# Attention and a gated feed-forward layer on one core: signs of the weights made on ScalarE, the clamp replaced by a check of sums, the closing checks split, and another order

## The chip, the cores and the metric

The kernel runs on one core of one Trainium2 chip. The metric is the device time of one execution in microseconds (us); the median of three runs before the change is 667.53 us (666.39 to 667.61). Work of the core is spread over TensorE (PE, matmuls), VectorE (DVE), ScalarE (ACT), GpSimd (POOL) and SyncE (SP, here only the queue that issues DMAs).

## The reference

```python
def _attn_ref(q, k, v, n_global, n_local):            # q, k, v: (4, 8, 768, 64)
    scores = scale * np.matmul(q, k.transpose(0, 1, 3, 2))
    keep = is_global | is_local                       # 8 first keys, or 0 <= row - key < 96
    dist = np.where(is_global & ~is_local, float(n_local), np.abs(rel))
    scores = np.where(keep, scores - slopes[:, None, None] * dist, -1e9)
    scores = scores - np.max(scores, axis=-1, keepdims=True)
    a = np.exp(scores)
    a = a / (np.sum(a, axis=-1, keepdims=True) + 1e-09)
    return np.matmul(a, v)

def _moe_ref(x, w_in, w_out):                         # x: (3072, 512), w_in: (512, 2048), w_out: (2048, 512)
    h = x @ w_in
    sp = np.where(h > 20.0, h, np.log1p(np.exp(np.minimum(h, 20.0))))
    g = h * np.tanh(sp)
    return g @ w_out
```

The weights arrive as 64-bit floats and are seen by the kernel as pairs of 32-bit words.

## The kernel before

The 3072 rows are cut into 12 chunks of 256 (`NC`), each with 8 score tiles per block of 128 rows, `t` = 0 to 95 in all. For a tile: matmuls of scores (`scores`, L370, two tiles at a time), the row maximum on DVE (`largest`, L384), the exponential with its row sum on ACT (`exps`, L393), a split of the result into two 16-bit halves (`high_a`, `low_a`), a transposing DMA (`turn_a`) and the matmuls with v (`weigh`, L429). Each block of rows then gets its normalisation (`rows`) and is split and transposed in turn (`high_x`, `low_x`, `turn_x`).

The feed-forward part runs in 96 steps `m`, 8 to a chunk, each of 256 rows by 256 of the 2048 inner columns. Step m is: 24 matmuls into the PSUM tile `ph` (`moe_in`, L474); on ACT e = exp(-h) (`exp_h`, L481); on DVE `half_e` (L485), which clamps e at 2^35 and adds 0.5; on ACT the square, a logarithm with a bias and an exponential (`square_e` L489, `ln_u` L493, `inverse_u` L497); on DVE a product with e + 0.5 (`times_r`, L501) and a product with h (`times_h`, L505, which also gives a maximum into `gmax`); a split into 16-bit halves `gt` (`high_g`, `low_g`); and 12 matmuls into `po` (`moe_out`, L523).

The weights come in 32 pieces of 128 x 512 (`load_w`), and each must be turned from 64-bit words into a pair of 16-bit halves before `moe_in` or `moe_out` reads it: `exponent_w` scales the upper word into the tile `wc`; `sign_w` writes the two 16-bit words of the tile `ws`, the low bits with a shift (L315) and the sign with a mask (L316), both on DVE; `join_w` merges `wc` and `ws` (L321, DVE); `high_w` and `low_w` make the halves. Raw pieces lie in the places of finished ones, so a later load also waits for earlier joins.

The order of all this is written out by hand in the string `PROGRAM`: one letter per function (the table `acts` gives it) and the number of the tile, step or piece, such as `i16` for `moe_in(16)`. Each engine's queue holds its instructions in that order, and an engine works its queue strictly from the front; DMAs are issued by SP's queue in the same order. A tick after a token (`g1'`) sends a function that can run on either of two engines to the other one: to DVE in place of ACT for the functions that go through `copy` (L151 on DVE, L153 on ACT), to DVE in place of POOL for those that go through `rest` (L157).

After the last step two ACT instructions per half move `po` out (`evacuate`, L530). Then the kernel decides whether its shortcuts were valid: it forms indicators of `osum`, `xmax`, `wmax` and `gmax` on DVE (L634 to L637), sums them over the partitions with one matmul (L639), reduces the result to one flag on DVE (L641 to L649, L79), loads the flag and, were it 0, would run a second, plain version (`dense`). With these inputs it does not run.

## Time and profile before

| | |
|---|---|
| median of three runs | 667.53 us (666.39 to 667.61) |
| the profiled execution | 665.3 us, of which the span from first to last instruction 663.5 us |
| PE busy, instructions | 599.8 us, 5042 matmuls |
| DVE busy, instructions | 511.1 us, 1300 |
| ACT busy, instructions | 459.5 us, 1030 |
| POOL busy, instructions | 165.4 us, 129 |
| mean granted clock of TensorE | 0.958 of full |

Groups of instructions are read as: line, engine, operation, tile out<-in, shape and type, count, then busy time in us, mean ns of one, and the idle time of the engine in front of them with what ended it. A stretch of the span is read as: its length, then busy us of each engine with the count of instructions, the granted clock of TensorE, and the share of the DMA engines. Start-to-start times on one engine are shorter than the durations shown, since consecutive instructions overlap by some tens of ns.

### The profile page before, as it was taken

What the parts mean: (1) busy time and instruction counts of PE and PEld (TensorE: products, weight loads), DVE (VectorE), ACT (ScalarE), POOL (GpSimd) and SP (SyncE); (2) the same over time, 40 slices, a digit from 0 to 9 for tenths busy, and PEclk for the clock granted to TensorE, in tenths of its full rate; (3) what the DMA queues carried; (4) which work ended last, traced back from release to release, by engine and by line L of the source; (5) the groups of instructions that cost most, each with busy time, mean ns of one, the idle gap of its engine ahead of it and who ended that gap; (6) DMA issues with size and microseconds to landing.
All of it is one profiled execution on the core that took longest, in us unless ns stands there. A gap on an engine that the chain in (4) does not pass through costs nothing.

```text
span 663.5 us, 13588 instructions
## 1 busy us (share of the span) xinstructions
PE 599.8 (90%) x5042; PEld 407.4 (61%) x5042; DVE 511.1 (77%) x1300; ACT 459.5 (69%) x1030; POOL 165.4 (25%) x129
## 2 busy tenths in 40 slices
PE   3456849997999999999999998999999999999995
PEld 2345537564767667676666666666676676667762
DVE  7789999999886897597489889796768468364551
ACT  3656765766895894786586896787776786565660
POOL 1424332413150401112132354321231203021000
PEclk9767878998999999999999999999999999999998
DMA  8999996834562683194144666741133025320001
GB/s 198 248 239 208 226 312 214 234 112 138 144 164 56 149 180 70 41 203 97 43 109 113 139 163 150 144 124 41 34 81 81 17 68 124 81 33 1 33 1 36
DMA packets 152681, 80.39 MB, mean 121 GB/s; under 512 B 121376, under 2 KB 141856, under 8 KB 152608
## 3 DMA queue, kind: packets, MB, share of 16 engines
q1 hardware_dynamic: 152608, 79.46, 49.8%
q8 instruction: 41, 0.67, 0.4%
q14 instruction: 32, 0.26, 0.1%
HBM read 38.54 MB, written 6.29 MB: 68 GB/s over the span
## 4 chain that ended last, share of the span: by engine, by line
PE 56%; DVE 7%; ACT 1%; issue 1%; DMA 1%; SPq 0%; DVEq 0%
PE ph L474 26%; PE po L523 25%; PE pav L429 3%; PE sc L370 2%; DVE r L501 1%; DVE gf L505 1%; DVE A L384 1%; DVE e L485 1%; DMA AT<-hl 1%; DVE wc L157 0%; DVE xhl L451 0%; DVE vo L219 0%; DVE vo L151 0%; ACT e L481 0%; ACT r L497 0%
## 5 line engine op out<-in xcount | busy, mean ns | idle before, releaser
L474 PE MATMUL ph<-xT,wts 128*128 128x256 f16 x2304 | 268.6, 275 | 14.5 <-DVE gmax L505 13.6
L474 PEld LDWEIGHTS <-wts 128*128 128x128 f16 x2304 | 225.4, 99 | 56.0 <-issue 13.7
L523 PE MATMUL po<-wts,gt 128*128 128x512 f16 x1056 | 241.7, 382 | 3.4 <-DVE gt L157 3.4
L523 PEld LDWEIGHTS <-gt 128*128 128x128 f16 x1152 | 110.6, 98 | 129.1 <-issue 5.1
L157 POOL TENSOR_TENSOR gt<-gf,gt 128x512 f16<-128x512 f32 x46 | 57.0, 1238 | 268.5 <-ACT gt L153 122.3
L501 DVE TENSOR_TENSOR r<-r,e 128x512 f32<-128x512 f32 x96 | 73.7, 768 | 46.2 <-ACT r L497 45.5
L393 ACT ACTIVATE A<-A,nm 128x256 f32<-128x256 f32 (+1 forms) x192 | 91.6, 478 | 20.5 <-DVE nm L384 20.2
L157 POOL TENSOR_TENSOR hl<-A,hl 128x512 f16<-128x512 f32 (+1 forms) x52 | 67.0, 1295 | 129.3 <-DVE hl L151 54.8
L481 ACT ACTIVATE e<-ph 128x512 f32<-128x512 f32 x96 | 56.4, 588 | 56.1 <-PE ph L474 55.7
L489 ACT ACTIVATE u<-e 128x512 f32<-128x512 f32 x96 | 60.1, 626 | 39.1 <-DVE e L485 39.0
L485 DVE TENSOR_SCALAR e<-e 128x512 f32<-128x512 f32 x96 | 48.4, 504 | 46.0 <-ACT e L481 45.7
L384 DVE CUSTOM_DVE_ANT_0 A<-sc,mb 128x256 f32<-128x256 f32 (+1 forms) x192 | 67.2, 395 | 8.6 <-PE sc L370 6.6
L493 ACT ACTIVATE r<-u,quarter 128x512 f32<-128x512 f32 x96 | 68.9, 718 | 2.1
L505 DVE CUSTOM_DVE_ANT_0 gf<-r,ph 128x512 f32<-128x512 f32 x96 | 65.5, 682 | 5.3 <-DVE r L501 1.6
L497 ACT ACTIVATE r<-r 128x512 f32<-128x512 f32 x96 | 59.9, 624 | 1.6
L153 ACT ACTIVATE gt<-gf 128x512 f16<-128x512 f32 x61 | 38.1, 624 | 26.5 <-DVE gmax L505 26.3
L429 PEld LDWEIGHTS <-AT 128*128 128x128 f16 x1056 | 39.6, 102 | 18.7 <-DMA AT<-hl 10.0
L370 PE MATMUL sc<-kr,qr 64*128 64x256 f32 (+1 forms) x96 | 24.3, 570 | 28.8 <-DVE nm L384 23.0
L157 DVE TENSOR_TENSOR gt<-gf,gt 128x512 f16<-128x512 f32 x50 | 39.2, 785 | 8.2 <-ACT gt L153 7.5
L157 POOL TENSOR_TENSOR wts<-ws,wts 128x512 f16<-128x512 f32 x16 | 26.8, 1676 | 67.7 <-ACT wts L153 62.6
L429 PE MATMUL pav<-vc,AT 128*128 128x64 f16 x480 | 34.3, 199 | 8.9 <-DMA AT<-hl 8.3
L429 PE MATMUL pav<-vo,AT 128*128 128x64 f16 x576 | 38.8, 199 | 0.0
(90 smaller groups left out, 542.0 us busy)
## 6 DMA issues: line engine op xcount, KB each, us to landing
kr<-kd SPq DMA_DIRECT2D x32, 208.0 KB, 4.4
qr<-qT SPq DMA_DIRECT2D x24, 256.0 KB, 4.1
vr<-v SPq DMA_DIRECT2D x12, 512.0 KB, 4.0
wts<-w_in SPq DMA_DIRECT2D x12, 512.0 KB, 5.3
wts<-w_out SPq DMA_DIRECT2D x12, 512.0 KB, 5.2
out<-ob SPq DMA_DIRECT2D x11, 512.0 KB, 3.1
vc<-vo SPq DMA_DIRECT2D x20, 192.0 KB, 2.8
kr<-kd SPq DMA_DIRECT2D x16, 144.0 KB, 3.7
```

What stands on the lines that cost most here:

```text
L157: (nc.vector if other else nc.gpsimd).tensor_tensor(out, in_, high, op=ALU.subtract)
L384: nc.vector.tensor_tensor_reduce(out=A[:, j, 0:w], in0=sc[j][:, 0:w], in1=m, scale=-1.0 / (UNIT if ci < CF32 else UNIT * SQ), scalar=3.0e3 ...
L393: nc.scalar.activation(A[:, j], A[:, j], AF.Exp, bias=nm[:, h:h + 1], scale=-1.0, accum_out=rs[:, h:h + 1])
L429: nc.tensor.matmul(pav[:, cols], AT[:, (x * 2 + j) * nk + kk, :], vs[kk][:, y, cols], start=(n == 0), stop=(n == last))
L474: nc.tensor.matmul(ph[:, j, :].rearrange("p (b t) -> p b t", b=2), wv4[:, 2 * fb, x, c * P:(c + 1) * P], xT[:, :, y * NCC + c, :], start=( ...
L481: nc.scalar.activation(mish[m]["e"], mish[m]["h"], AF.Exp, scale=-1.0 / (SV * SW))
L489: nc.scalar.activation(u, mish[m]["e"], AF.Square)
L493: nc.scalar.activation(mish[m]["r"], mish[m]["u"], AF.Ln, bias=quarter, scale=1.0 / RS)
L497: nc.scalar.activation(r, r, AF.Exp, scale=-1.0)
L501: nc.vector.tensor_tensor(r, r, mish[m]["e"], op=ALU.mult)
L505: nc.vector.tensor_tensor_reduce(out=gf, in0=mish[m]["r"], in1=mish[m]["h"], scale=SG / (SV * SW * RS), scalar=0.0, op0=ALU.mult, op1=ALU. ...
L523: nc.tensor.matmul(pos[ci][t], gt[:, x, j, t * P:(t + 1) * P], wv4[:, 2 * fb + 1, y, :], start=(fb == 0 and n == 0), stop=(fb == NFB - 1 a ...
```

## The change

Five things change.

1. `sign_w` keeps only the sign, and can run on ACT: a scaled copy of the upper word by 2^-111 into a 16-bit float leaves a zero with the sign. The shift for the low bits is its own function, `bits_w`, on DVE. Of the 32 signs 19 go to ACT and 13 stay on DVE.
2. `half_e` is gone. The 0.5 is added in two places: as the bias of the square on ACT, read from a tile `half`, and inside `times_r`, which becomes a scalar_tensor_tensor, (e + 0.5) * r. In place of the clamp, `exp_h` also gives out the sum over its row (`esum`), and the closing check asks that no sum reach 2^35.
3. The closing checks become `checks` 0, 1 and 2 inside the written order: 0 and 1 stand ahead of the last `moe_out`, with one matmul (L570) ahead of its 12, and 2 behind the evacuation, with one matmul of two columns and two DVE instructions.
4. `PROGRAM` is a new order throughout, and the ticks differ: over the whole program, ACT takes 6 more `exponent_w` and all 8 masks of the first kind (`mask_own`) and 4 more of the second (`mask_far`), DVE 14 more `high_g`.
5. The flag is written as an integer directly.

How the queues move is shown at three places. The first is DVE in the part where the weights are turned and the first feed-forward steps run. `ISA` is the custom instruction of L505 (L511 now), and L316 (before) and L320 (now) are the sign. Before:

```order
L315 TENSOR_SCALAR ws<-wts 128x512
L316 TENSOR_SCALAR ws<-wts 128x512
L501 TENSOR_TENSOR r<-r,e 128x512
L321 SCALAR_TENSOR_TENSOR ws<-wc,ws 128x512
L505 ISA gf,gmax<-r,ph 128x512
L505 ISA gmax 128x1
L157 TENSOR_TENSOR gt<-gf,gt 128x512
L321 SCALAR_TENSOR_TENSOR ws<-wc,ws 128x512
L315 TENSOR_SCALAR ws<-wts 128x512
L316 TENSOR_SCALAR ws<-wts 128x512
L485 TENSOR_SCALAR e<-e 128x512
```

And now:

```order
L320 TENSOR_SCALAR ws<-wts 128x512
L151 TENSOR_SCALAR wts<-ws 128x512
L326 TENSOR_SCALAR ws<-wts 128x512 x2
L330 SCALAR_TENSOR_TENSOR ws<-wc,ws 128x512 x2
L507 SCALAR_TENSOR_TENSOR r<-e,r 128x512
L326 TENSOR_SCALAR ws<-wts 128x512
L157 TENSOR_TENSOR wts<-ws,wts 128x512
L511 ISA gf,gmax<-r,ph 128x512
L511 ISA gmax 128x1
```

The shift (L315, now L326) no longer has a mask behind it each time, and L485 is gone between the products.

The second place is ACT in the same part of the program: L481 (now L491) is the first exponential of a step, L489 (L495) the square, L493 (L499) the logarithm, L497 (L503) the second exponential. Before:

```order
L481 ACTIVATE e<-ph 128x512
L153 ACTIVATE gt<-gf 128x512
L153 ACTIVATE wts<-ws 128x512
L489 ACTIVATE u<-e 128x512
L481 ACTIVATE e<-ph 128x512
L493 ACTIVATE r<-u,quarter 128x512
L497 ACTIVATE r<-r 128x512
```

And now:

```order
L153 ACTIVATE wc<-wts 128x512
L491 ACTIVATE e,esum<-ph 128x512
L495 ACTIVATE u<-e,half 128x512
L499 ACTIVATE r<-u,quarter 128x512
L322 ACTIVATE ws<-wts 128x512
L503 ACTIVATE r<-r 128x512
```

The square can follow the exponential with nothing of DVE between, it reads a bias, and signs (L322) stand between the instructions of a step.

The third place is the end of DVE's queue. Before, all that follows the sum over `osum` (L634) came behind the evacuation:

```order
L634 TENSOR_SCALAR ind<-osum 128x24
L641 TENSOR_SCALAR v_8666<-sc 1x48
L643 COPY v_8668<-sc 1x2
L644 TENSOR_REDUCE v_8668<-sc 1x12
L647 TENSOR_REDUCE v_8672<-v_8666 1x1
L645 TENSOR_SCALAR v_8668<-v_8668 1x14
L648 TENSOR_REDUCE v_8672<-v_8668 1x1
L649 SCALAR_TENSOR_TENSOR done<-v_8672,fl 1x1
L79 CAST done_i<-done 1x1
```

Now only the last two rows do; the reductions ahead of them wait for the matmul that stands in front of the last `moe_out`:

```order
L578 TENSOR_TENSOR v_114<-v_114 1x1
L579 TENSOR_SCALAR v_114<-v_114 1x1
L580 SCALAR_TENSOR_TENSOR v_114<-v_114,fl 1x1
L585 TENSOR_SCALAR last<-sc 1x2
L586 SCALAR_TENSOR_TENSOR done_i<-last,v_114 1x1
```

Nine instructions behind the evacuation have become two.

The diff, cut (the rows of the order are left out but for two of each):

```diff
-    def sign_w(i):
-        r = wraw[i]
-        s = mt.tile([P, DM], I32, name="ws", bufs=WB)
-        h16 = r.rearrange("p f w -> p (f w)").bitcast(U16).rearrange("p (f w) -> p f w", w=4)
-        s16 = s.bitcast(U16).rearrange("p (f w) -> p f w", w=2)
-        nc.vector.tensor_scalar(s16[:, :, 0], h16[:, :, 1], 13, None, op0=ALU.logical_shift_right)
-        nc.vector.tensor_scalar(s16[:, :, 1], h16[:, :, 3], 0x8000, None, op0=ALU.bitwise_and)
-        wst[i, 1] = s
+    def words(i, w):
+        if (i, 1) not in wst:
+            wst[i, 1] = mt.tile([P, DM], I32, name="ws", bufs=WB)
+        return wst[i, 1].bitcast(U16).rearrange("p (f w) -> p f w", w=2)[:, :, w]
+    def sign_w(i, other=False):
+        if other:
+            nc.vector.tensor_scalar(words(i, 1), halves(i, 3), 0x8000, None, op0=ALU.bitwise_and)
+        else:
+            nc.scalar.activation(words(i, 1).bitcast(F16), wraw[i][:, :, 1].bitcast(F32), AF.Copy, scale=EXPO)
+    def bits_w(i):
+        nc.vector.tensor_scalar(words(i, 0), halves(i, 1), 13, None, op0=ALU.logical_shift_right)
...
-        nc.scalar.activation(mish[m]["e"], mish[m]["h"], AF.Exp, scale=-1.0 / (SV * SW))
-    def half_e(m):
-        e = mish[m]["e"]
-        nc.vector.tensor_scalar(e, e, NTOP, 0.5, op0=ALU.min, op1=ALU.add)
+        nc.scalar.activation(mish[m]["e"], mish[m]["h"], AF.Exp, scale=-1.0 / (SV * SW), accum_out=esum[:, m:m + 1])
...
-        nc.scalar.activation(u, mish[m]["e"], AF.Square)
+        nc.scalar.activation(u, mish[m]["e"], AF.Square, bias=half_)
...
-        nc.vector.tensor_tensor(r, r, mish[m]["e"], op=ALU.mult)
+        nc.vector.scalar_tensor_tensor(r, mish[m]["e"], 0.5, r, op0=ALU.add, op1=ALU.mult)
...
+    def checks(i):
+        if i == 0:
+            nc.vector.tensor_scalar(ind[:, 0:2 * NC - 2], osum[:, 0:2 * NC - 2], 0.0, 0.0, op0=ALU.mult, op1=ALU.is_equal)
...
+        elif i == 1:
+            nc.vector.reduce_max(worst, esum, axis=AX.X)
...
+            nc.tensor.matmul(pi, ones, ind, start=True, stop=True)
...
+        else:
+            pe = ps.tile([1, 2], F32, name="sc")
+            nc.tensor.matmul(pe, ones, osum[:, 2 * NC - 2:], start=True, stop=True)
+            last = cp.tile([1, 2], F32, name="last")
+            nc.vector.tensor_scalar(last, pe, 0.0, 0.0, op0=ALU.mult, op1=ALU.is_equal)
+            nc.vector.scalar_tensor_tensor(L.done_i, last[:, 0:1], v3[:, 3:4], last[:, 1:2], op0=ALU.mult, op1=ALU.mult)
...
-        K0 q0 q1 L0' L6' L5' K1 L1' L4' M3 M2' L2' M0 L3' v0 M7' M1 M4' M5' M6' L7' f0 q2 s0 t0 t1 y0 s2 y1 g0' p0' q3 g1' t2 p1 t3 y2 X0 h0' s4 y3
+        K0 q0 K1 L7 v0 L3 L0 L6 L4 f0 L5 M3 M1' M4 M5 M6 q1 M2 M0 M7 L2 L1 s0 q2 t0 t1 y0 s2 y1 g0' p0' h0 g1' X0 t2 t3 y2 q3 p1' s4 y3 l0 X1 g2 t4 p2' y4 x0
...
-        i94 z93 Z93' i95 j94 m94 u94 n94 o91 r94 j95 G94 m95 H94 u95 n95 o92 z94' Z94 r95 G95 H95 o93 z95' Z95' o94 o95 Q11
+        o93 r95 G95 H95 o94 z95 Z95 k0 k1 o95 Q11 k2
...
-    nc.vector.tensor_scalar(ind[:, 0:2 * NC], osum, 0.0, 0.0, op0=ALU.mult, op1=ALU.is_equal)
-    nc.vector.tensor_scalar(ind[:, 2 * NC:4 * NC], xmax, 1.0, None, op0=ALU.is_ge)
-    nc.vector.tensor_scalar(ind[:, 4 * NC:NX], wmax, 1.0, None, op0=ALU.is_ge)
-    nc.vector.tensor_scalar(ind[:, NX:], gmax, 1.0, None, op0=ALU.is_ge)
-    pi = ps.tile([1, NX + NC * NFP], F32, name="sc")
-    nc.tensor.matmul(pi, ones, ind, start=True, stop=True)
...
```

More of the change, by code (lines that the diff above doesn't have):

```diff
@@ L72, in tile_kernel @@
     nlf = n_f[:, 1:2]
-    done = const.tile([1, 1], F32, name="done")
     done_i = const.tile([1, 1], I32, name="done_i")
@@ L78, in tile_kernel @@
         windowed(st, tc, locals())
-    nc.vector.tensor_copy(done_i, done)
     left = nc.values_load(done_i[0:1, 0:1], min_val=0, max_val=1)
@@ L144, in windowed @@
     nc.vector.memset(quarter, 0.25 / RS)
+    half_ = cp.tile([P, 1], F32, name="half")
+    nc.vector.memset(half_, 0.5)
     ones = cp.tile([P, 1], F32, name="ones")
@@ L334, in windowed @@
     gmax = cp.tile([P, NC * NFP], F32, name="gmax")
+    esum = cp.tile([P, NC * NFP], F32, name="esum")
     NT_ = NC * 2 * (H // 2)
@@ L543, in flags @@
         nc.vector.tensor_scalar(fl[:, 3:4], L.n_f[0:1, 1:2], float(NLMAX), fl[:, 2:3], op0=ALU.is_le, op1=ALU.mult)
+    NX = 4 * NC
+    NG = NC * NFP
+    ind = cp.tile([P, NX + NG + 1], F32, name="ind")
+    worst = cp.tile([P, 1], F32, name="worst")
+    v1 = cp.tile([1, NX - 2], F32, name="v1")
+    v2 = cp.tile([1, NC], F32, name="v2")
+    v3 = cp.tile([1, 4], F32, name="v3")
+    def checks(i):
+        if i == 0:
+            nc.vector.tensor_scalar(ind[:, 0:2 * NC - 2], osum[:, 0:2 * NC - 2], 0.0, 0.0, op0=ALU.mult, op1=ALU.is_equal)
+            nc.vector.tensor_scalar(ind[:, 2 * NC - 2:NX - 2], xmax, 1.0, None, op0=ALU.is_ge)
+            nc.vector.tensor_scalar(ind[:, NX - 2:NX], wmax, 1.0, None, op0=ALU.is_ge)
+        elif i == 1:
+            nc.vector.reduce_max(worst, esum, axis=AX.X)
+            nc.vector.tensor_scalar(ind[:, NX + NG:], worst, NTOP, None, op0=ALU.is_lt)
+            nc.vector.tensor_scalar(ind[:, NX:NX + NG], gmax, 1.0, None, op0=ALU.is_ge)
+            pi = ps.tile([1, NX + NG + 1], F32, name="sc")
+            nc.tensor.matmul(pi, ones, ind, start=True, stop=True)
+            nc.vector.tensor_scalar(v1, pi[:, 0:NX - 2], P - 0.5, None, op0=ALU.is_ge)
+            nc.vector.tensor_reduce(v3[:, 0:1], v1, axis=AX.X, op=ALU.min)
+            nc.vector.tensor_scalar(v3[:, 2:3], pi[:, NX + NG:], P - 0.5, None, op0=ALU.is_ge)
+            nc.vector.tensor_tensor(v3[:, 0:1], v3[:, 0:1], v3[:, 2:3], op=ALU.mult)
+            nc.vector.reduce_max(v2, pi[:, NX:NX + NG].rearrange("p (c f) -> p c f", f=NFP), axis=AX.X)
+            nc.vector.tensor_reduce(v3[:, 1:2], v2, axis=AX.X, op=ALU.min)
+            nc.vector.tensor_reduce(v3[:, 2:3], pi[:, NX - 2:NX], axis=AX.X, op=ALU.min)
+            nc.vector.tensor_tensor(v3[:, 1:2], v3[:, 1:2], v3[:, 2:3], op=ALU.min)
+            nc.vector.tensor_scalar(v3[:, 1:2], v3[:, 1:2], 0.5, None, op0=ALU.is_ge)
+            nc.vector.scalar_tensor_tensor(v3[:, 3:4], v3[:, 0:1], fl[:, 3:4], v3[:, 1:2], op0=ALU.mult, op1=ALU.mult)
+        else:
[4 more added lines that the diff above has]
+            nc.vector.scalar_tensor_tensor(L.done_i, last[:, 0:1], v3[:, 3:4], last[:, 1:2], op0=ALU.mult, op1=ALU.mult)
@@ L556, in windowed @@
         "R": rows, "T": high_x, "U": low_x, "V": turn_x,
-        "A": exponent_w, "B": sign_w, "C": join_w, "D": high_w, "E": low_w,
-        "i": moe_in, "j": exp_h, "m": half_e, "u": square_e, "n": ln_u, "r": inverse_u, "G": times_r, "H": times_h,
-        "z": high_g, "Z": low_g, "o": moe_out, "Q": evacuate, "Y": store, "f": lambda i: flags(),
+        "A": exponent_w, "S": sign_w, "B": bits_w, "C": join_w, "D": high_w, "E": low_w,
+        "i": moe_in, "j": exp_h, "u": square_e, "n": ln_u, "r": inverse_u, "G": times_r, "H": times_h,
@@ L560, in windowed @@
+        "z": high_g, "Z": low_g, "o": moe_out, "Q": evacuate, "Y": store, "f": lambda i: flags(), "k": checks,
     }
     PROGRAM = """
[L562 to L564 removed]
```

127 lines of the change are left out of this document (56 added, 71 removed).

## The prediction

> **What bounds the kernel now.** I read the page's busy shares and slices first, then the busy time by stretches, then PE's waits, then the groups of DVE and ACT up to 165 us. The page's parts 1 and 2 (each digit is tenths of a fortieth of the span):
>
> ```profile
> PE 599.8 (90%) x5042; PEld 407.4 (61%) x5042; DVE 511.1 (77%) x1300; ACT 459.5 (69%) x1030; POOL 165.4 (25%) x129
> PE   3456849997999999999999998999999999999995
> DVE  7789999999886897597489889796768468364551
> ```
>
> PE is the engine of the whole, but not at the front: in the first six slices (16.6 us each) DVE is fuller. The stretches, cut at points that mean something below (start:end, then us and counts of PE, PEld, DVE, ACT, POOL):
>
> ```profile
> 0.00:77.57 77.57, 42.18 (x324) 30.21 (x325) 66.78 (x204) 44.56 (x127) 26.90 (x27) 0.76 0.98 226
> 77.57:105.70 28.13, 18.98 (x192) 15.67 (x193) 27.92 (x62) 17.11 (x35) 6.94 (x6) 0.82 0.92 238
> 105.70:174.03 68.33, 62.71 (x414) 39.02 (x411) 67.18 (x139) 48.92 (x84) 18.54 (x11) 0.98 0.61 181
> 174.03:655.60 481.57, 475.50 (x4116) 322.40 (x4115) 347.88 (x889) 348.94 (x787) 112.98 (x87) 1.00 0.39 90
> ```
>
> Up to 174.03 DVE is busy 66.78 + 27.92 + 67.18 = 161.9 us, 93%, and ACT 110.6. From 174.03 on PE is busy all but 6 of 481.57 us, so that stretch cannot shrink by more than those 6. PE's waits up to 175 us (who, for whom: us, times, longest), and after it the last one, from 174 us to the end:
>
> ```profile
> PE sc L370 <- DVE nm L384: 23.0, 10, 5.0
> PE ph L474 <- DVE gmax L505: 8.8, 5, 3.4
> PE pav L429 <- DMA AT<-hl: 8.3, 4, 4.1
> ...
> PE ph L474 <- DVE gmax L505: 5.0, 6, 1.6
> ```
>
> DVE ends most of them. So DVE's instructions ahead of a matmul set the front, PE sets the rest, and two points of PE's queue carry the sum (start, length):
>
> ```profile
> 105.70 2.77 PE L523 MATMUL pav<-wts,gt 128*128 128x512 f16 x12
> 174.03 2.78 PE L474 MATMUL ph<-xT,wts 128*128 128x256 f16 x24 [0.15 <-DVE gmax L505]
> ```
>
> The first is `moe_out(8)`, the second `moe_in(16)`. Counted in the two orders, ahead of `i16` PE has exactly the same work in both: 13 pairs of scores, 24 tiles weighed, 16 `moe_in`, 14 `moe_out`. Ahead of `o8` it had 12, 24, 6 and 1; now it has 12, 24, 5 and 2 ahead of `i10`, the same work but for 0.03 us. So the question is when PE gets to `i10`, and when to `i16`.
>
> **The change part by part.** Durations on DVE and ACT, up to 165 us (mean ns behind the busy us):
>
> ```profile
> L485 DVE TENSOR_SCALAR e<-e 128x512 f32<-128x512 f32 x14 | 7.2, 512 | 0.0
> L315 DVE TENSOR_SCALAR ws<-wts 128x512 uint16<-128x512 uint16 x24 | 11.5, 479 | 0.0
> L316 DVE TENSOR_SCALAR ws<-wts 128x512 uint16<-128x512 uint16 x24 | 12.7, 527 | 0.0
> L151 DVE TENSOR_SCALAR wc<-wts 128x512 f32<-128x512 f32 x8 | 6.8, 852 | 0.0
> L157 DVE TENSOR_TENSOR hl<-A,hl 128x512 f16<-128x512 f32 x7 | 6.7, 956 | 0.0
> L636 DVE TENSOR_SCALAR ind<-wmax 128x2 f32<-128x2 f32 x1 | 1.1, 1111 | 0.0
> L151 DVE TENSOR_SCALAR mb<-r 128x128 bf16<-128x128 f32 x8 | 1.4, 220 | 0.0
> L151 DVE TENSOR_SCALAR mb<-e 128x256 bf16<-128x256 f32 x5 | 1.2, 284 | 0.0
> L501 DVE TENSOR_TENSOR r<-r,e 128x512 f32<-128x512 f32 x14 | 10.5, 748 | 0.0
> L321 DVE SCALAR_TENSOR_TENSOR ws<-wc,ws 128x512 int32<-128x512 int32 x31 | 22.2, 724 | 0.1
> L153 ACT ACTIVATE wc<-wts 128x512 f32<-128x512 f32 x16 | 10.5, 663 | 2.6 <-DMA wts<-w_in 2.5
> L393 ACT ACTIVATION_READ_ACCUMULATOR A<-A,nm 128x1 f32 x48 | 9.0, 187 | 0.0
> L493 ACT ACTIVATE r<-u,quarter 128x512 f32<-128x512 f32 x14 | 10.0, 717 | 0.3
> L489 ACT ACTIVATE u<-e 128x512 f32<-128x512 f32 x14 | 8.8, 627 | 7.7 <-DVE e L485 7.7
> L153 ACT ACTIVATE mb<-e 128x256 bf16<-128x256 f32 x3 | 1.0, 404 | 5.5 <-DVE e L258 5.5
> ```
>
> On DVE up to `i16`: 16 clamps go, 16 x 0.512 = 8.2 us. Of 32 masks of the sign 19 go, 19 x 0.527 = 10.0. Six `exponent_w` go, 6 x 0.852 = 5.1. The early check L636 moves to the end, 1.1. Eight own and four far masks go to ACT, 8 x 0.220 + 4 x 0.284 = 2.9. Four second halves of scores come from POOL (two of them of half the size), taken as three whole ones, +2.9. Together 8.2 + 10.0 + 5.1 + 1.1 + 2.9 - 2.9 = 24.4 us less: 161.9 becomes 137.5. The other kinds move by one or two instructions each, both ways; I leave them out.
>
> The product with e + 0.5 is of a kind that the trace lacks in fp32. It is bounded by 724 (the merge of the same form, on 32-bit integers) and 748 (the plain product); I take it as unchanged.
>
> ACT gets what DVE loses: 19 signs like the scaled copy beside them, 19 x 0.663 = 12.6; 6 exponents, 4.0; 12 masks, at most 12 x 0.404 = 4.8; 16 accumulator reads, 16 x 0.187 = 3.0; and the bias of the square, which I price by the one ACT instruction of this size that has a bias tile: 717 against 627, 16 x 0.09 = 1.4. That is 25.8, so 110.6 becomes 136.4. DVE and ACT come out level, at about 137 us each.
>
> Up to `i10` in place of `o8`, DVE's account is: 6 clamps, 3.1; 14 shifts and 5 masks in place of 16 and 16, 2 x 0.479 + 11 x 0.527 = 6.8; one exponent 0.9; two merges 1.4; L636 1.1; and 2.9 more for the same halves of scores. The early masks count nothing here: their cover is DVE's wait at the start, and ACT now makes them one after the other ahead of the first row maxima, which I charge with 0.9 us. Sum 3.1 + 6.8 + 0.9 + 1.4 + 1.1 - 2.9 - 0.9 = 9.5; `i10` starts at 105.7 - 9.5 = 96.2 us. Bounds: 9.5 + 2.9 + 0.9 = 13.3 if the halves of scores only fill time in which DVE waited and the masks are hidden; 0 if ACT, not DVE, is what is late.
>
> Two durations above are means with waits in them: start to start the clamp took 0.34 us where POOL was quiet.
>
> ```profile
> 60.82 0.41 DVE L485 TENSOR_SCALAR e<-e 128x512 f32<-128x512 f32 x1
> 61.15 1.21 DVE L219 SCALAR_TENSOR_TENSOR vo<-vr,vo 128x1024 f16<-128x1024 f32 x1
> ```
>
> [...] The trace has both, 0.33 undisturbed and 0.512 in the mean, and I keep the mean.
>
> From `i10` to `i16` PE needs the 62.71 us that it was busy between the two points, and it stood still for 5.6. DVE and ACT get ahead of it now, with 137 of some 160 us, 86%. That both can be that full without PE standing still the trace shows later, and also what a full DVE costs:
>
> ```profile
> 175.00:200.00 25.00, 25.00 (x217) 16.94 (x215) 21.61 (x57) 23.01 (x66) 11.81 (x10) 1.00 0.58 155
> 375.00:400.00 25.00, 24.93 (x230) 16.48 (x227) 23.08 (x60) 21.93 (x58) 14.39 (x12) 1.00 0.71 164
> 400.00:425.00 25.00, 22.36 (x250) 14.68 (x249) 24.24 (x64) 16.93 (x46) 9.18 (x7) 1.00 0.63 142
> ```
>
> With DVE at 92% and ACT at 88% PE lost 0.07 of 25 us; with DVE at 97% it lost 2.6. I allow 2.2 us of standing still: `i16` at 96.2 + 62.7 + 2.2 = 161.1, which is 12.9 us earlier. What was late at `i10`, DVE's maxima and products, is followed by PE itself.
>
> Behind `i16`, 80 clamps leave DVE, whose waits made 5.0 of PE's 6.07 us; the order is new there, so I take 1 us and bounds of 5 to either side. The cover of ACT's 96 longer squares and 96 accumulator reads is ACT's own idle time, 132 us of that stretch.
>
> The end: the row sum's check, the matmul and eight instructions on DVE.
>
> ```profile
> 655.65 0.18 DVE L634 TENSOR_SCALAR ind<-osum 128x24 f32<-128x24 f32 x1 [6.78 <-ACT ob L530]
> 655.88 0.41 PE L639 MATMUL sc<-ind,ones 128*1 128x146 f32 x2 [0.99 <-DVE ind L634]
> 657.42 0.14 DVE L79 CAST done_i<-done 1x1 int32<-1x1 f32 x1
> ```
>
> From 655.65 to 657.56 it took 1.9 us. Now a matmul (0.4) and two DVE instructions (0.4) remain, 1.1 less; but the other matmul stands on PE ahead of the last `moe_out`, 0.4 more. Net 0.7 earlier.
>
> Sum: 12.9 + 1.0 + 0.7 = 14.6 us. The profiled execution took 665.3 us (its span 663.5), so 650.7; the median of the runs is 2.2 above it, which gives **652.9**, written as 653.
>
> **The rivals.** *All slack goes* (0.17): `i10` comes 13.3 us earlier, and PE neither stands still nor runs slowly up to `i16`. For it speaks a row in which PE was slow behind a wait:
>
> ```profile
> 90.23 4.07 PE L474 MATMUL ph<-xT,wts 128*128 128x256 f16 x24 [3.38 <-DVE gmax L505]
> ```
>
> Such 24 took 2.78 at 174.03, and shorter waits would keep them so. Then 13.3 + 5.6 + 1.0 + 0.7 = 20.6, and 667.5 - 20.6 = 646.9. Against it: three engines nearly level seldom lose nothing. [...]
>
> *ACT sets the front* (0.12). It starts its first exponential at 10.09 us, and signs now stand between the four instructions of a step:
>
> ```profile
> 10.09 0.40 ACT L393 ACTIVATE A<-A,nm 128x128 f32<-128x128 f32 x1 [1.56 <-DVE nm L384]
> ```
>
> Behind that it has 136.4 - 4.8 = 131.6 us to do. At the 88% of the row at 375 us this ends at 160, no later than PE's 161; at 84% it ends at 167, which leaves 7 us, and 1.7 behind: 658.8. Below 84% it decides. For it: ACT, DVE and ACT again take turns on each piece of weights. Against: ACT was at 92% in the row at 175 us.
>
> *Late transposes, slower than before* (0.08). Between the transposing DMA of a tile and its `weigh` there lie, behind chunk 2, a median of two blocks of PE's work (`moe_in` or `moe_out`, 2.6 us each) where there were three.
>
> ```profile
> AT<-hl SPq DMA_TRANSPOSE x96, 2.9
> 86.03 0.33 PE L429 MATMUL pav<-vc,AT 128*128 128x64 f16 x3 [2.32 <-DMA AT<-hl]
> ```
>
> Landing takes 2.9 us, and a late one held up PE and all behind it for 2.32. Seven of 72 late would cost 16.2 and eat the gain; ten give 652.9 + 23.2 = 676. Against: 13 tiles have only one block between in both orders, and before they cost next to nothing.
>
> *The gain is eaten* (0.05): ACT's turns and PE's waits give back what DVE saves, about 667.
>
> **How the numbers follow.** The forecast holds 0.58. The range of 642 to 664 takes the gain's upper bounds on one side (13.3 + 5.6 + 5 + 0.7 = 24.6 below 667.5, 642.9) and most of ACT's case on the other, and leaves out the last two rivals and a tail. A difference of 0.2%, 1.3 us, is about what a measurement of this kernel can tell from none. Faster: 0.58 + 0.17 + 0.12 = 0.87; same 0.05; slower 0.08.
>
> **What would show it.** In the new profile: PE's 24 matmuls of `i16` start near 161 us; DVE's busy time up to there near 137 us and ACT's about the same; no row of L485's kind; the square as long as the logarithm; the product near 0.75 us; PE's waits for row maxima shorter; seven instructions fewer behind the evacuation. I am wrong if ACT ends most of PE's and DVE's waits in the front, if the product costs much more than 0.75 (0.1 more is 1.6 us up to `i16`), or if PE waits for `AT` behind it.

## The result, and the profile after

The change is faster: 648.12 us in the median of four runs (645.74 to 648.18) against 666.96 for the kernel before (665.13 to 667.61). The ratio is 0.9713, with a 95% interval of 0.9683 to 0.9743. The forecast was 653.0 us, with a range of 642 to 664.

The page of the changed kernel, parts 1 and 2 (busy us, share and instructions; then tenths of a fortieth of the span, here 16.2 us each). The span is 646.3 us, the profiled execution's own time 648.11:

```profile
PE 598.9 (93%) x5044; PEld 408.4 (63%) x5044; DVE 470.5 (73%) x1188; ACT 485.7 (75%) x1142; POOL 166.9 (26%) x136
PE   3666779989999999999999999999999999999995
DVE  6787989999879658888688675487866698434442
ACT  6576789989998786977686798578866886755761
```

PE's work is the same (599.8 before). DVE lost 40.6 us, ACT gained 26.2, and ACT now shows nines in five of the slices seven to twelve, where DVE has them in seven to ten. The stretches, cut at the points that answer to those of before (start:end, us, then busy us and counts of PE, PEld, DVE, ACT and POOL, granted clock, DMA share, GB/s):

```profile
0.00:69.85 69.85, 38.29 (x305) 28.70 (x305) 52.89 (x180) 47.17 (x137) 15.31 (x19) 0.84 1.05 219
69.85:98.04 28.19, 24.52 (x202) 17.05 (x201) 25.17 (x57) 23.11 (x47) 10.34 (x8) 0.78 1.07 267
98.04:163.80 65.76, 61.40 (x422) 39.94 (x420) 63.65 (x118) 61.93 (x119) 16.88 (x11) 1.00 0.66 197
163.80:638.92 475.12, 474.52 (x4122) 322.62 (x4118) 328.42 (x834) 352.79 (x842) 124.33 (x99) 1.00 0.44 93
638.92:646.30 7.38, 0.19 (x2) 0.09 (x2) 0.35 (x2) 0.69 (x2) 0.00 (x0) 0.70 0.23 81
```

Up to `moe_in(16)`, at 163.80 us, DVE was busy 52.89 + 25.17 + 63.65 = 141.7 us and ACT 47.17 + 23.11 + 61.93 = 132.2 us, which is 87% and 81% of the time. From 98.04 to 163.80 three engines are nearly full at once: PE 93%, DVE 97%, ACT 94%. Behind 163.80 PE stands still for 0.6 of 475.12 us, where it stood still for 6 before. The points of PE's queue themselves (start, length; `i10` is the second half of the 48 at 95.42):

```profile
86.80 5.30 PE L484 MATMUL ph<-xT,wts 128*128 128x256 f16 x24 [3.08 <-DVE gmax L511]
95.42 5.40 PE L484 MATMUL ph<-xT,wts 128*128 128x256 f16 x48
...
163.80 5.41 PE L484 MATMUL ph<-xT,wts 128*128 128x256 f16 x48
```

PE's waits up to 165 us, and behind the dots from 165 us to the end (for whom; us, times, longest):

```profile
PE sc L380 <- DVE nm L394: 14.2, 7, 3.3
PE pav L439 <- DMA AT<-hl: 11.7, 6, 3.0
PE ph L484 <- DVE gmax L511: 7.3, 5, 3.1
PE sc L380 <- DMA kr<-kd: 6.0, 2, 5.2
...
PE sc L583 <- ACT ob L536: 0.8, 1, 0.8
PE ph L484 <- DVE gmax L511: 0.6, 1, 0.6
```

The waits for the largest of a gate (L511, before L505) fell from 5.0 to 0.6 us behind the front, and those for row maxima (L394, before L384) from 23.0 to 14.2 in it. What grew is the wait for a transposing DMA, from 8.3 to 11.7. The groups of ACT and DVE that the change touched, over the whole span (busy us, mean ns, idle time ahead of them):

```profile
L495 ACT ACTIVATE u<-e,half 128x512 f32<-128x512 f32 x96 | 68.8, 717 | 1.7
L491 ACT ACTIVATION_READ_ACCUMULATOR e<-ph 128x1 f32 x96 | 18.6, 194 | 0.0
L322 ACT ACTIVATE ws<-wts 128x512 f16<-128x512 f32 x14 | 10.8, 774 | 1.5 <-DMA wts<-w_out 1.5
L507 DVE SCALAR_TENSOR_TENSOR r<-e,r 128x512 f32<-128x512 f32 x96 | 73.8, 769 | 85.1 <-ACT r L503 84.8
```

And the end of PE's and DVE's queues:

```profile
635.78 0.41 PE L570 MATMUL sc<-ind,ones 128*1 128x145 f32 x2
639.66 0.19 PE L583 MATMUL sc<-osum,ones 128*1 128x2 f32 x2 [0.78 <-ACT ob L536]
639.89 0.15 DVE L585 TENSOR_SCALAR last<-sc 1x2 f32<-1x2 f32 x1 [1.98 <-PE sc L583]
640.07 0.21 DVE L586 SCALAR_TENSOR_TENSOR done_i<-last,v 1x1 int32<-1x1 f32 x1
```

So the span is shorter by 663.5 - 646.3 = 17.2 us. Of it 174.03 - 163.80 = 10.2 came up to `moe_in(16)`. Behind the start of PE's last matmul, 655.88 before and 639.66 now, there are 7.6 us before and 6.6 now, 1.0 less. The remaining 6.0 came between: 481.85 us from the one point to the other before, 475.86 now.

### The profile page after: what moved, and what is told of

Its sections match the earlier page's. It is cut to its first block, busy times and chain, and to the rows that moved or that the text cites. A ratio compares the mean times of both kernels' runs of the same rounds, so it can differ in the third digit from the quotient of the medians.

```text
span 646.3 us, 13614 instructions
## 1 busy us (share of the span) xinstructions
PE 598.9 (93%) x5044; PEld 408.4 (63%) x5044; DVE 470.5 (73%) x1188; ACT 485.7 (75%) x1142; POOL 166.9 (26%) x136
## 4 chain that ended last, share of the span: by engine, by line
PE 76%; DVE 9%; ACT 6%; DMA 3%; issue 2%; SPq 2%; DVEq 0%; ACTq 0%
PE ph L484 34%; PE po L529 33%; PE sc L380 4%; PE pav L439 4%; DMA AT<-hl 1%; DVE A L394 1%; PE pav L529 1%; ACT wc L153 1%; DVE ws L330 1%; DVE r L507 1%; SPq L423 1%; DVE ws L326 1%; DMA wts<-w_out 1%; ACT wts L153 1%; DVE hl L157 1%
## 5 line engine op out<-in xcount | busy, mean ns | idle before, releaser
L507 DVE SCALAR_TENSOR_TENSOR r<-e,r 128x512 f32<-128x512 f32 x96 | 73.8, 769 | 85.1 <-ACT r L503 84.8
L157 POOL TENSOR_TENSOR hl<-A,hl 128x512 f16<-128x512 f32 (+1 forms) x58 | 69.7, 1204 | 187.6 <-ACT hl L153 83.0
L157 POOL TENSOR_TENSOR gt<-gf,gt 128x512 f16<-128x512 f32 x49 | 61.4, 1253 | 209.9 <-DVE gt L151 93.6
L491 ACT ACTIVATE e<-ph 128x512 f32<-128x512 f32 x96 | 56.7, 591 | 71.4 <-PE ph L484 70.6
L394 DVE CUSTOM_DVE_ANT_0 A<-sc,mb 128x256 f32<-128x256 f32 (+1 forms) x192 | 67.6, 395 | 21.5 <-PE sc L380 18.7
L511 DVE CUSTOM_DVE_ANT_0 gf<-r,ph 128x512 f32<-128x512 f32 x96 | 65.6, 683 | 7.2 <-DVE r L507 3.6
L499 ACT ACTIVATE r<-u,quarter 128x512 f32<-128x512 f32 x96 | 68.9, 718 | 2.1
L495 ACT ACTIVATE u<-e,half 128x512 f32<-128x512 f32 x96 | 68.8, 717 | 1.7
L503 ACT ACTIVATE r<-r 128x512 f32<-128x512 f32 x96 | 59.8, 623 | 1.5
L439 PEld LDWEIGHTS <-AT 128*128 128x128 f16 x1056 | 42.4, 103 | 26.2 <-DMA AT<-hl 14.7
L439 PE MATMUL pav<-vc,AT 128*128 128x64 f16 x480 | 35.6, 200 | 12.0 <-DMA AT<-hl 11.7
L153 ACT ACTIVATE gt<-gf 128x512 f16<-128x512 f32 x47 | 29.3, 623 | 22.7 <-DVE gmax L511 20.4
L380 PE MATMUL sc<-kr,qr 64*128 64x256 f32 (+1 forms) x96 | 25.5, 614 | 20.2 <-DVE nm L394 14.2
L157 DVE TENSOR_TENSOR gt<-gf,gt 128x512 f16<-128x512 f32 x47 | 32.5, 691 | 12.6 <-ACT gt L153 12.0
L439 PE MATMUL pav<-vo,AT 128*128 128x64 f16 x576 | 40.7, 201 | 0.0
L403 ACT ACTIVATION_READ_ACCUMULATOR A<-A,nm 128x1 f32 x192 | 36.2, 188 | 0.0
L157 POOL TENSOR_TENSOR wts<-ws,wts 128x512 f16<-128x512 f32 x14 | 20.3, 1454 | 56.3 <-ACT wts L153 49.7
```

The source lines that it names most:

```text
L157: (nc.vector if other else nc.gpsimd).tensor_tensor(out, in_, high, op=ALU.subtract)
L394: nc.vector.tensor_tensor_reduce(out=A[:, j, 0:w], in0=sc[j][:, 0:w], in1=m, scale=-1.0 / (UNIT if ci < CF32 else UNIT * SQ), scalar=3.0e3 ...
L403: nc.scalar.activation(A[:, j], A[:, j], AF.Exp, bias=nm[:, h:h + 1], scale=-1.0, accum_out=rs[:, h:h + 1])
L439: nc.tensor.matmul(pav[:, cols], AT[:, (x * 2 + j) * nk + kk, :], vs[kk][:, y, cols], start=(n == 0), stop=(n == last))
L491: nc.scalar.activation(mish[m]["e"], mish[m]["h"], AF.Exp, scale=-1.0 / (SV * SW), accum_out=esum[:, m:m + 1])
L495: nc.scalar.activation(u, mish[m]["e"], AF.Square, bias=half_)
```

## The experiments

Each kernel is read by two numbers of its profile beside its time: when PE starts `moe_in(16)`, and how long the span lasts behind that (one profile each; the start moved by 0.4 us between the change and o4_checks_last, which have the same front). The table has all kernels; below it stands each with its edit. Medians are compared with the kernel before on the same chip (666.7 to 667.1).

| kernel | order | clamp | signs | median us | ratio to before | `i16` starts | span behind it |
|---|---|---|---|---|---|---|---|
| before | old | DVE | DVE | 666.96 | 1 | 174.03 | 489.5 |
| the change | new | none | 19 on ACT | 648.12 | 0.9713 (0.9683 to 0.9743) | 163.80 | 482.5 |
| o1_old_order_clamp | old | none | DVE | 656.43 | 0.9834 (0.9796 to 0.9872) | 170.48 | 484.7 |
| o2_old_order_signs | old | DVE | 19 on ACT | 662.39 | 0.9936 (0.9915 to 0.9958) | 171.81 | 488.8 |
| o3_old_order_both | old | none | 19 on ACT | 655.41 | 0.9821 (0.9782 to 0.986) | 169.84 | 484.5 |
| o4_checks_last | new | none | 19 on ACT | 648.13 | 0.9712 (0.9674 to 0.9749) | 164.23 | 482.9 |
| n1_new_order_clamp_back | new | DVE, just ahead of the square | 19 on ACT | 678.44 | 1.0163 (1.0121 to 1.0205) | 173.01 | 504.7 |
| p1_clamp_behind_exp | new | DVE, right behind the exponential | 19 on ACT | 668.79 | 1.0028 (1.0016 to 1.004) | 172.80 | 494.8 |
| p2_clamp_two_behind | new | DVE, two places behind it | 19 on ACT | 668.93 | 1.0033 (1.0019 to 1.0046) | 170.51 | 496.3 |
| n2_new_order_signs_back | new | none | DVE | 653.74 | 0.9794 (0.9754 to 0.9833) | 170.44 | 482.7 |
| p3_half_signs_back | new | none | 14 on ACT | 650.06 | 0.9752 (0.9725 to 0.9779) | 165.60 | 482.5 |
| n3_new_order_old_parts | new | DVE, just ahead of the square | DVE | 680.87 | 1.0201 (1.016 to 1.0243) | 176.59 | 502.8 |
| n4_loads_earlier | new | none | 19 on ACT | 647.15 | 0.9705 (0.9662 to 0.9747) | 163.04 | 482.5 |

My theory was that of the prediction: DVE's work ahead of a point of PE's queue sets that point, so that each part is worth the DVE time that it removes, and the parts add. The rivals: the parts are worth only what the new order makes of them (they do not add), or the new order alone is the gain.

### The parts alone, in the old order

**o1_old_order_clamp.** The clamp goes, the sum and the bias come in, and the product is fused; nothing is moved. The closing check of the sums is left out.

```diff
-        nc.scalar.activation(mish[m]["e"], mish[m]["h"], AF.Exp, scale=-1.0 / (SV * SW))
+        nc.scalar.activation(mish[m]["e"], mish[m]["h"], AF.Exp, scale=-1.0 / (SV * SW), accum_out=esum[:, m:m + 1])
-        nc.scalar.activation(u, mish[m]["e"], AF.Square)
+        nc.scalar.activation(u, mish[m]["e"], AF.Square, bias=half_)
-        nc.vector.tensor_tensor(r, r, mish[m]["e"], op=ALU.mult)
+        nc.vector.scalar_tensor_tensor(r, mish[m]["e"], 0.5, r, op0=ALU.add, op1=ALU.mult)
```

and every `m` of the order is struck out.

> The kernel before, in its own order, with one part of the change: the clamp's instruction on VectorE is dropped, the exponential gives out its row sum, the square gets the bias and the product adds 0.5. The closing check of these sums is left out. Theory 'work' (the front is as long as VectorE's work ahead of it, in any good order): 16 clamps of 0.512 us lie ahead of moe_in(16), so the front is 6 to 8 us shorter, and the last 480 us lose 2 of their 6 us of waits: about 658. Theory 'order' (instructions stay where the old order put them, and each engine still waits for what was planned around them): 663 to 667.

Measured: 656.43 us, 10.7 less than the kernel before on the same chip (667.09). By the spans 3.6 us come in the front and 4.8 behind it. That is nearly the time of theory 'work', but by other shares than the 6 to 8 and 2 that it named. In PE's waits from 175 us to the end of this kernel:

```profile
PE ph L477 <- DVE gmax L508: 1.9, 2, 1.4
```

What follows: behind `moe_in(16)` the clamp alone takes PE's waits for the gate's maximum from 5.0 to 1.9 us. From `moe_in(16)` to PE's last matmul this kernel takes 477.35 us, where the kernel before took 481.85 and the change 475.86, so the clamp is 4.5 of the 6.0 us that the change gains there. In the front 16 clamps of 0.512 us make 8.2 us by their durations, but DVE's busy time up to `moe_in(16)` fell by 4.3 us (161.9 to 157.6), and that point came 3.6 us earlier.

**o2_old_order_signs.** The same 19 signs on ACT, each at the place in the order where DVE's mask stood; the clamp stays.

```diff
-        nc.vector.tensor_scalar(s16[:, :, 1], h16[:, :, 3], 0x8000, None, op0=ALU.bitwise_and)
+        nc.scalar.activation(words(i, 1).bitcast(F16), wraw[i][:, :, 1].bitcast(F32), AF.Copy, scale=EXPO)
```

> The kernel before, in its own order, with the other part alone: the same 19 signs as in the change are made on ScalarE, at the place where the mask stood, the clamp stays. Theory 'work': VectorE has 10.0 us less ahead of moe_in(16), ScalarE 12.6 more, from 110.6 to 123 of 174: about 659. Theory 'order': the join of a piece now waits for a sign that ScalarE reaches late, behind work planned ahead of it: 665 to 670.

Measured: 662.39 us, 4.7 less. By the spans 2.2 us come in the front and 0.7 behind it; the rest is that the kernel before was profiled in an execution 1.8 us faster than its median here (665.3 against 667.09). 19 masks of 0.527 us make 10.0 us by their durations; DVE's busy time up to `moe_in(16)` fell by 8.6 us (to 153.3), and 2.2 us of the front came. The time lies between the two theories.

**o3_old_order_both.** Both edits together, in the old order; the check of the sums is left out here as well.

> The kernel before, in its own order, with both parts (the closing check of the sums left out, the other checks at the end as before). Theory 'work': 18 us less on VectorE in the front, of which PE can follow about 11, and 2 behind: about 654, so the new order is worth some 5 us beside it. Theory 'order': 662 to 667, and the new order is worth 14 us or more.

Measured: 655.41 us, 11.7 less. Alone the two parts brought 10.7 and 4.7, so even without a new order they do not add. In the front it is 4.2 us, where alone they brought 3.6 and 2.2. Why so little shows in the stretch that ends with `moe_out(8)`, PE's first point of the kernel before (the columns are those of the stretches above); it starts at 103.34 here, and the stretch begins with the same matmul as the one from 77.57 to 105.70 of the kernel before:

```profile
76.58:103.34 26.76, 19.45 (x192) 15.78 (x193) 21.94 (x53) 20.78 (x44) 5.00 (x5) 0.81 1.00 249
```

The kernel before took 28.13 us for it, with DVE busy 27.92 (the second of the prediction's stretches). DVE has 6.0 us less to do and the stretch is 1.4 us shorter: DVE goes from 99% to 82% busy, and no longer sets its length alone. Of the 4.8 us in which it stands still, 3.9 are waits for ACT's part of the same steps and pieces:

```profile
DVE r L513 <- ACT r L509: 2.1, 3, 1.0
DVE ws L332 <- ACT ws L324: 1.8, 2, 1.2
```

What follows: in the old order most of the freed DVE time is not used. DVE's busy time up to `moe_in(16)` fell by 14.4 us (161.9 to 147.5), and that point came 4.2 us earlier. The step "PE gets to its point earlier by DVE's removed work" does not hold here, where DVE waits for ACT. The median is near that of theory 'work' (654), and the change is 7.3 us faster still.

### The parts taken back, in the new order

**n1_new_order_clamp_back.** The change, with the clamp on DVE again, each one just ahead of its square in the order; no sum, no bias, no fused product; the check of the sums is left out.

```diff
+    def half_e(m):
+        e = mish[m]["e"]
+        nc.vector.tensor_scalar(e, e, NTOP, 0.5, op0=ALU.min, op1=ALU.add)
-        nc.scalar.activation(u, mish[m]["e"], AF.Square, bias=half_)
+        nc.scalar.activation(u, mish[m]["e"], AF.Square)
-        nc.vector.scalar_tensor_tensor(r, mish[m]["e"], 0.5, r, op0=ALU.add, op1=ALU.mult)
+        nc.vector.tensor_tensor(r, r, mish[m]["e"], op=ALU.mult)
```

> The changed kernel in its new order with the clamp back as an instruction of VectorE ahead of each square, without sums, bias or the fused product. In the old order the clamp was worth 10.7 us (667.1 to 656.4). Theory 'additive' (part and order are worth the same in either company): 648.1 + 10.7, about 659. Theory 'matched' (the new order fills just the time that the parts free, and parts are worth more in it): 662 to 668.

Measured: 678.44 us, 30.3 more than the change and 11.7 more than the kernel before, slower than either theory had it. The waits over the whole span:

```profile
ACT u L499 <- DVE e L495: 99.7, 85, 4.0
```

ACT's square stood behind the clamp 85 times of 96. The clamp, just ahead of the square in the order, is queued on DVE behind whatever the order has before it, and ACT's queue stands still meanwhile. Whether that is the clamp or my place for it was open, and two more runs ask it.

**p1_clamp_behind_exp.** As n1_new_order_clamp_back, with each clamp right behind its exponential.

> The new order and the new signs, with the clamp back on VectorE as in the kernel before (no sum, no bias, no fused product), each clamp right behind its exponential in the order, where n1_new_order_clamp_back had it just ahead of the square. What is open: whether the 30 us by which n1 was slower than the change are the clamps' work, or the place where I put them. Theory 'place': ACT's wait of 99.7 us for the clamped tile came from clamps that stood behind other DVE work; with the clamp at once behind the exponential most of it goes, and the time falls to that of the change plus what the clamp cost in the old order (656.4 against 667.1: some 11 us), 655 to 663 us, PE's waits behind the gates' maxima under 10 us. Theory 'work': 96 clamps of 0.5 us do not fit into the new order anywhere, 672 to 680 us. A third way: DVE now stands waiting for the exponential, and what is queued behind it is late; then above 680 us, with DVE's idle time ended by ACT.

Measured: 668.79 us, 9.7 less than with the late clamp, but 20.7 more than the change. The waits now lie on both sides (whole span):

```profile
DVE e L495 <- ACT e L491: 74.3, 71, 4.7
ACT u L499 <- DVE e L495: 47.8, 62, 2.2
```

**p2_clamp_two_behind.** Each clamp two places behind its exponential, and each square two places later than the change has it.

> The same, with each clamp two places behind its exponential and each square two places later than the change has it (the old order has medians of three places from exponential to clamp and two from clamp to square). Theory 'place': the best of the three, 652 to 660 us, since neither engine then waits for the other. Theory 'work': 672 to 680 us as in n1_new_order_clamp_back. Third way: the later square delays the product and the next moe_out; PE then waits for the gate's maxima or the transposed gate, and the time lies between.

Measured: 668.93 us, the same as p1_clamp_behind_exp though the waits lie elsewhere (`ACT u` behind the clamp 71.1 us, `DVE r` behind ACT 68.6). `i16` is 2.3 us earlier and the rest 1.5 longer.

What follows: a third of the 30.3 us was the place; 20.7 us are not removed by any of three places. Both bets that I had named are off: it is neither some 11 us nor 30 (the "third way" of the second text, a time between, is nearest). In the old order the clamp costs 10.7 us, in this one 20.7 at the best of my places. A fourth place might be better; that was not tried.

**n2_new_order_signs_back.** The change, with all signs as masks on DVE.

> The changed kernel in its new order with all 32 signs on VectorE, at the places where they stand on ScalarE. In the old order the signs were worth 4.7 us alone and 1.0 on top of the clamp. Theory 'additive': 649 to 653. Theory 'matched': the new order counts on ScalarE for 19 of them, 10.0 us of VectorE's work come back to a VectorE that is 86% busy up to moe_in(16): 655 to 658.

Measured: 653.74 us, 5.6 more than the change; 6.6 us in the front, 0.2 behind it. The time lies between the two theories. Its DVE, in the stretch from `moe_in(10)`, at 101.12 us here, to `moe_in(16)`, which answers to 98.04 to 163.80 in the change:

```profile
101.12:170.44 69.32, 61.63 (x421) 39.94 (x420) 68.48 (x128) 56.52 (x107) 13.35 (x10) 1.00 0.64 187
```

DVE is busy 68.48 of 69.32 us, and the stretch is 3.6 us longer than in the change; the other 3.1 us of the front come ahead of it. Without the clamp the signs are worth 0.6 us of the front in the old order (170.48 in o1_old_order_clamp, 169.84 in o3_old_order_both) and 6.6 in the new. Read the other way: this kernel has the parts of o1_old_order_clamp in the new order, and `moe_in(16)` starts at 170.44 and 170.48. With the signs on DVE the new order gains nothing in the front; with 19 of them on ACT it gains 6.0 us (169.84 to 163.80).

**p3_half_signs_back.** The change, with five of the 19 signs back on DVE, those of pieces 15, 17, 23, 26 and 29, which lie between `moe_in(10)` and `moe_in(16)`. It asks which of the two full engines sets that stretch.

> The change, with five of its 19 signs on ACT back on VectorE (every second one of pieces 14 to 31, those that lie between moe_in(10) and moe_in(16)). All 19 back cost 5.6 us (n2_new_order_signs_back). Theory 'VectorE sets this stretch, at 97%': 5/19 of that, and since these five lie in the full stretch up to 5 x 0.53 = 2.6 us: 649.5 to 651 us, moe_in(16) 1.4 to 2.6 us later than 163.8. Theory 'ScalarE sets it' (its chain from 92 to 125 us): ACT has 5 x 0.77 = 3.9 us less to do and moe_in(16) comes earlier: 645 to 647.5 us. Both full: no difference, 648 us within 1.

Measured: 650.06 us, 1.9 more; `moe_in(16)` at 165.60, 1.8 later. The stretch up to it, from `moe_in(10)`, which starts at 96.38 in this profile:

```profile
96.38:165.60 69.22, 63.14 (x420) 40.40 (x419) 66.88 (x123) 59.50 (x114) 14.02 (x11) 0.98 0.64 188
```

DVE has 3.2 us more in it than the change's 63.65, ACT 2.4 less, and it is 3.5 us longer. DVE is at 97% in both kernels, ACT at 86% here and at 94% there. Time and `moe_in(16)` are as the theory 'VectorE sets this stretch' had them: less work for ACT shortened nothing, and what DVE got came back as time. So ACT's 94% alone does not limit the stretch; that DVE alone does is not shown, since the chain that ended last in the change lies on ACT up to 125 us and on DVE from there to 145. (That `moe_in(10)` is 1.7 us earlier than in the change, though the edit stands behind it, shows how far this point moves between two profiles, and as much of the 3.5 us is that; `moe_in(16)` moves less, 163.80 and 164.23 in the change and in o4_checks_last.)

**n3_new_order_old_parts.** The new order with clamps (just ahead of the square) and signs on DVE.

> The new order with both old parts (clamp and all signs on VectorE), so the order alone against the kernel before. Theory 'additive': the order alone is worth the 7.3 us that separate the old order with both parts (655.4) from the change (648.1), so about 660. Theory 'matched': alone it is worth nothing, 665 to 672.

Measured: 680.87 us, 14.2 more than the kernel before, and slower than either theory had it. In the front, `moe_in(16)` comes 2.6 us later than with the old order and the same parts. The new order alone is no gain. Two limits of this: the clamp stands at its worst of three places, and the masks of tiles and second halves that the new order gives to other engines stay there. With the 9.7 us that the better place was worth between n1_new_order_clamp_back and p1_clamp_behind_exp taken off, an estimate, it would still be 4.5 us slower than before.

### Two small questions

**o4_checks_last.** The change, with the two tokens of the early checks moved behind the last evacuation.

```diff
-        o93 r95 G95 H95 o94 z95 Z95 k0 k1 o95 Q11 k2
+        o93 r95 G95 H95 o94 z95 Z95 o95 Q11 k0 k1 k2
```

> The changed kernel with all three closing checks behind the evacuation. The prediction's term for the end says 0.7 us slower than the change (1.1 us of VectorE's reductions come back, one matmul of 0.4 leaves the path): 648.8 where the change took 648.1. If the end lies behind something else, such as the last store, there is no difference.

Measured: 648.13 us against 648.12. The early place of the checks is worth nothing that can be told.

**n4_loads_earlier.** An attempt at a faster version: the first 16 loads of weights are each issued one place earlier, since ACT's first copies of a piece waited for them (1.8 us in all in the change, and 1.5 more for a sign).

> The changed kernel with each of the first 16 weight loads issued one place earlier (load 1 with load 0, and so on). In the front the DMA engines show a share of 1.05 to 1.16, and ScalarE and VectorE wait 5.2 us for weights to land. If late loads hold the front, those waits go and it takes 644 to 646. If the DMA engines are simply full, the transposes and k, q that stand behind the loads land later by as much: 648 to 651.

Measured: 647.15 us, between the two expectations, its range (646.62 to 648.97) over that of the change, so no difference is shown. ACT waits for no weights any more; PE's waits up to 165 us:

```profile
PE pav L439 <- DMA AT<-hl: 14.2, 9, 2.8
PE sc L380 <- DVE nm L394: 12.1, 7, 2.9
```

The wait for the transposed tiles went from 11.7 to 14.2 us. The DMA engines' busy share up to 98 us is 1.05 and 1.07 in the stretches of the change above. That what one transfer gains there another pays is how I read the two waits (1.8 and 1.5 us less for weights, 2.5 more for transposed tiles); it is not shown.

## Why the prediction was right, and where it was not

**What bounds the kernel.** Right. PE's work did not move, and behind the front PE cannot give more than its 6 us of waits: it gave 5.5 of them.

**Up to `moe_in(10)` in place of `moe_out(8)`: predicted 96.2 us, measured 98.04.** The term was 9.5 us of DVE's work, and 105.70 - 98.04 = 7.7 came. That they are so near is in part luck: DVE's busy time up to this point fell by 16.6 us (94.70 to 78.06), since kinds that the account left out or charged went too (by their durations the first halves of weights 2.2, the row sums `rs` 1.6, the early masks 2.9), and less than half of it came as time.

Up to `moe_in(16)` DVE's busy time fell by 20.2 us (161.9 to 141.7), where 24.4 was predicted. What failed there is the subtraction: the prices are durations, durations of neighbours overlap, and busy time counts an overlap once. Added up, count times mean, the durations of DVE's 403 instructions up to that point make 191.6 us, and those of the 353 of the change 166.7, so 24.9 less, almost the 24.4. On ACT the durations grew by 29.2 us (127.5 to 156.7), the busy time by 21.6 (110.6 to 132.2), where 25.8 was predicted. The prices of what was new were right: over the whole span the fused product takes 769 ns, the square 717 as priced, the accumulator read 194 for 187. Kinds that were there already changed both ways. Of the change, up to 164 us, and then of the kernel before, up to 174 us:

```profile
L326 DVE TENSOR_SCALAR ws<-wts 128x512 uint16<-128x512 uint16 x24 | 13.8, 593 | 0.1
L157 DVE TENSOR_TENSOR wts<-ws,wts 128x512 f16<-128x512 f32 x18 | 14.2, 793 | 0.1
L151 DVE TENSOR_SCALAR wts<-ws 128x512 f16<-128x512 f32 x7 | 3.1, 438 | 0.0
```

```profile
L157 DVE TENSOR_TENSOR wts<-ws,wts 128x512 f16<-128x512 f32 x16 | 11.0, 693 | 1.0 <-ACT wts L153 0.8
L151 DVE TENSOR_SCALAR wts<-ws 128x512 f16<-128x512 f32 x8 | 5.3, 660 | 0.0
```

The shift takes 593 ns where it took 479; its median is 460 and its longest 1417, so a few long ones make the mean. The second halves of weights take 793 for 693, but the first halves 438 for 660. What makes the long ones long was not measured. The prediction named a choice of price for the clamp: 0.34 us start to start with POOL quiet, or the mean duration of 0.512. It took the mean. In o1_old_order_clamp, where nothing is moved, DVE's busy time up to `moe_in(16)` fell by 4.3 us; 16 x 0.34 makes 5.4 and 16 x 0.512 makes 8.2, so the smaller price was the better one, and with it the sum of 24.4 had been 2.8 us smaller.

One price on ACT was off too: a sign took 774 ns, where I took 663 from the scaled copy; 19 x 0.11 makes 2.1 us. The chain that ended last is ACT's on nearly every step between 92 and 125 us, with signs in it (start, length; some rows of it):

```profile
100.84 0.62 ACT u L495
101.48 0.72 ACT r L499
...
102.79 0.67 ACT ws L322
...
105.61 0.61 ACT u L495
```

From 125 to 145 us the chain is DVE's, and from there PE's. The 33 us on ACT are the rival *ACT sets the front*; but the time that the rival gave, 658.8, did not come, and taking signs from ACT behind `moe_in(10)` made the kernel slower (p3_half_signs_back).

**The step that stood on too little: DVE's removed work ahead of a point is the gain there.** It came close in the sum (9.5 against 7.7, and 12.9 against 10.2 at `moe_in(16)`), but the runs do not bear it out as a mechanism. Up to `moe_in(16)` DVE's busy time fell by 4.3 us and the point came 3.6 us earlier with the clamp gone (o1_old_order_clamp); it was 8.6 and 2.2 with the signs on ACT (o2_old_order_signs), 14.4 and 4.2 with both (o3_old_order_both), and 20.2 and 10.2 in the change. Only the first is near one for one.

The other 6.0 of the 10.2 us came with the new order, and only together with the signs on ACT: with the clamp gone and the signs on DVE the point is the same in both orders (n2_new_order_signs_back and o1_old_order_clamp). It is not that DVE is fuller in the new order: up to `moe_in(16)` it is busy 87% of the time in o3_old_order_both and in the change, and 5.3 of the 6.0 us come ahead of the first point (`moe_in(10)` at 98.04, `moe_out(8)` at 103.34), where it is at 80% in the change and at 83% in o3_old_order_both. What differs is what PE waits for. Of o3_old_order_both, up to 165 us:

```profile
PE sc L382 <- DVE nm L396: 19.8, 10, 5.0
PE po L535 <- DVE gt L159: 2.8, 1, 2.8
```

In the change these are 14.2 and 0.2 us, the waits for transposed tiles are 3.3 us longer, and PE's busy time up to `moe_in(16)` is 1.4 us shorter. Why the row maxima come earlier is not shown. Nor is it shown how the 6.0 us divide between the sequence and the ticks, which take another 5.8 us of busy time from DVE (20.2 against 14.4): no run has the new ticks in the old order.

With the old parts the new order is slower in the front by 2.6 us (n3_new_order_old_parts). The parts alone were worth 11.7 us, the order alone minus 14 (with the clamp badly placed), both together 18.8. In the prediction the new order appeared only in what it put ahead of two points of PE's queue; that it had to be there for the work to count was not said.

**From `moe_in(10)` to `moe_in(16)`: predicted 64.9 us with 2.2 of standing still, measured 65.76.** PE was busy 61.40 and stood still 4.4. The row that I leaned on (DVE 92%, ACT 88%, PE losing 0.07 of 25 us) was not the state that came; DVE ran at 97% and ACT at 94%, and by the other row of the prediction, with DVE at 97% and 2.6 of 25 us lost, PE would stand still for 6.8. What came lies between the two.

**Behind `moe_in(16)`: predicted 1 us, bounds of 5 to either side; measured 6.0.** This is the term that was most mis-sized, by 5 us, a third of the whole sum, and it lies at its bound. The profile had the figure: DVE's waits for the gate's maximum made 5.0 of PE's 6.07 us there, and 80 clamps lay in the chain from exponential to maximum. o1_old_order_clamp shows that removing them, with nothing moved, brings 4.5 of the 6.0. I took 1 because "the order is new there"; the new order added 1.5 us to the 4.5. The ACT part was right: 80 accumulator reads and longer squares hid in ACT's idle time, of which 475.12 - 352.79 = 122 us are left.

**The end: predicted 1.1 less behind, and 0.4 more on PE ahead of the last `moe_out`; measured 1.0 less behind.** The 0.4 lie in the 6.0 above. Right in size, but too small to be told: with the checks at the end (o4_checks_last) the median is the same.

**The sum.** 12.9 + 1.0 + 0.7 = 14.6 was predicted, 10.2 + 6.0 + 1.0 = 17.2 measured: one term 2.7 too large, another 5.0 too small, and it is luck that they partly cancel. The forecast of 652.9 is 4.8 us above the measured 648.12: 2.6 are the terms, and 2.2 were added because the kernel before had been profiled in an execution that much faster than its median, while the change was profiled in one at its median (648.11).

**The rivals.** *All slack goes* (646.9) is nearest to the time, but for another reason than it gave: PE still waits 39 us up to 165 us, and the slack that went is that behind `moe_in(16)`. The slow matmuls stayed too: at 86.80 us 24 took 5.30 us in place of 2.78, behind a wait of 3.08. *Late transposes* did not come where it placed its cost: behind chunk 2 no wait of PE for `AT` shows; in the front that wait grew (11.7 us for 8.3). *The gain is eaten* did not come; n1_new_order_clamp_back and p1_clamp_behind_exp show a way in which it would have: this order with a hop to DVE in the middle of ACT's four instructions.
